# A decode step of attention and a gated feed-forward: which engine issues the loads

## The chip, the cores and the metric

The kernel runs on one core of a Trainium2 chip. The core has TensorE (PE, matrix products), VectorE (DVE), ScalarE (ACT), GpSimd (POOL) and SyncE (SP), which run side by side and wait for each other through semaphores, and 16 DMA engines, which move data between main memory (HBM) and the on-chip memory. Any of SP, ACT and POOL can issue a transfer. The metric is the device time of one execution in microseconds (us).

## The reference

One token (batch 1, width 512) goes through two branches that are mixed by a gate: attention with 32 query heads over a cache of 8 key and value heads, 32768 positions each, and a gated feed-forward of width 1792. All is float32.

```python
B, Sq, D = 1, 1, 512
Hq, Hkv, Sk, Dh = 32, 8, 32768, 128
F = 1792

g = sigmoid((x * gate_w).sum(-1, keepdims=True))
q = (x @ wq).reshape(B, Sq, Hq, Dh).transpose(0, 2, 1, 3)
k, v = repeat(k_cache, 4, axis=1), repeat(v_cache, 4, axis=1)
p = softmax(einsum("bhqd,bhkd->bhqk", q, k) * Dh ** -0.5)
a = einsum("bhqk,bhkd->bhqd", p, v).transpose(0, 2, 1, 3).reshape(B, Sq, Hq * Dh) @ wo
b = (silu(x @ w1) * (x @ w3)) @ w2          # x is A_x
out = g * a + (1 - g) * b
```

## The kernel before, in words

**Units.** The key cache and the value cache are each cut into 16 units. A K unit is a quarter of two heads, a V unit is half of one head; either is 128 partitions by 64 KB, 8.39 MB. I call them K0 to K15 and V0 to V15. The weights wq and wo are of the same size, w1, w3 and w2 have 3.67 MB each; wo is loaded in six parts, of 16, 7, 4, 2, 2 and 1 of its 32 columns of blocks.

**Buffers.** Nearly all of the on-chip memory is in two buffers of one unit each, `big_a` (the buffer number 0 in the code, with halves A0 and A1) and `big_b` (1, with B0 and B1), and in `aside`, three quarters of half a unit. wq goes to `big_a`, K0 and K2 to `big_b`, all other K units to `big_a`. V0 to V11 go to `big_b`, V12 and V14 to `big_a`, V13 and V15 to `big_b`, wo to `big_a`, w2 to the place of `aside`.

**The stages.** First q is computed from wq, spread over TensorE, and turned into `win`. Then a loop over t from 0 to 15 takes in one K unit a turn: ScalarE copies part of the unit to `aside` (`set_aside`, so that `big_a` comes free before the unit is worked up), VectorE transposes it in eight pieces of 128x2048 (L367), TensorE multiplies each piece by q (`scores_part`, L351), ScalarE copies the scores out. After every fourth K unit the scores of two heads are complete: they are transposed on TensorE (`turn`), and `softmax` finds the maximum on VectorE and takes the exponential on ScalarE (`probs`). From t = 4 (`LAG`) on, the same turn also takes V unit v = t - 4: TensorE multiplies it by its probabilities (`values_all`, L452). In the turn t = 3 the products with w1 and w3 are made. After the loop V12 to V15 follow (`load_unit`, `values`, L575), the weights of the heads (`norm`, `place`, `own_head`), then the products with wo (`wide`, L631, and `ff_down`, L662) and with w2 (`down`, on VectorE, L638), and two small stores of the result.

**How the order is made.** The program is written by a small planner of the kernel's own. `pr.add(engine, ...)` appends an operation to the engine's list; it derives from the names that the operation reads and writes which earlier operations it must wait for, and gives it a semaphore to raise. Each engine goes through its own list in the order in which it was written. Every load goes through `load` (L194), except V0 to V11 (`load_values`, L433); both put it on SP's list. A load by `load` raises one of nine semaphores (`lane`), taken in turn.

**TensorE's loop.** The other engines' lists are written out flat, but TensorE runs a real loop over the units. It therefore can't wait for ever higher counts: it waits for a fixed count and takes it off again (`take`). Such a semaphore is a *credit*. The load of V0 to V11 raises the credit "values" by 16 when it has landed, and TensorE does `take("values", 16)` before `values_all`.

**SP's list**, in order: wq, K0, K1, K2, K3, w1, w3, K4, V0, K5, V1, and so on in turn to K15, V11; then V12, V13, V14, V15, w2, the six parts of wo, and one of the two stores. ACT issues the two small rows x and gate_w and the other store. POOL's list: 34 short operations, nearly all of which make masks and constants at the start; the last of these turns the gate into 1 - gate (L302). One more `memset` (L537), in the last turn of the loop, clears `otp`, where the attention's output is laid out for the product with wo.

Of the kernel before, what the change touches and what calls it, by code (L numbers as in the profile page):

```python
# [114 lines left out]
def kernel(  # L115
# [12 lines left out]
    nc = tc.nc  # L128
# [5 lines left out]
    NC = D // P  # L134
# [8 lines left out]
    NP = HKV // 2  # L143
    NH = 4 * NP
# [5 lines left out]
    pr = Program(nc, nc.alloc_semaphore)  # L150
    pr.semaphore("stored")
    pe, dve, act, pool = (
        lambda fn, _e=e, **kw: pr.add(_e, fn, **kw) for e in ("PE", "DVE", "ACT", "POOL")
    )
    V, A, T = nc.vector, nc.scalar, nc.tensor

    def sbuf(name, *shape):
        return nc.alloc_sbuf_tensor(name, [P, *shape], F32)[:]

    fold = sbuf("fold", 32)  # L160
    big = [sbuf("big_a", 2 * R), sbuf("big_b", 2 * R)]
# [19 lines left out]
    otp = kt[1][:, 0:1024].rearrange("p (k c) -> p k c", c=32)  # L181
# [5 lines left out]

    lanes = [0]

    def load(dst, src, writes, over=()):  # L190
        lanes[0] += 1
        lane = f"load{lanes[0] % 9}"
        return pr.add(
            "SP", lambda: nc.sync.dma_start(dst, src), writes=writes, over=[*over, lane], inc=lane, by=16, also=lane,  # L194
        )

    def region(b, z):
# [2 lines left out]

    for i, t in enumerate((x.rearrange("a b n -> (a b) n"), gate_w.rearrange("(o n) -> o n", o=1))):
        pr.add("ACT", lambda i=i, t=t: nc.scalar.dma_start(rows[i][0:1, :], t), writes=[f"row{i}"], inc="row", by=16)
    load(big[0], wq.rearrange("(p c) n -> p (c n)", c=NC), ["A0", "A1"])
    opened = pr.ops["SP"].pop()
    first_load = opened.fn()
    first_load.then_inc(pr.semaphore(opened.inc[0]), opened.inc[1])
# [11 lines left out]
    high, top = sbuf("high", 1), sbuf("top", 32)  # L218
    G = nc.gpsimd
# [45 lines left out]
    def clear(**kw):  # L265
        pe(zeros,
           reads=["acc"], writes=["s"], **kw)
# [15 lines left out]
    for c in range(NC):  # L283
        def part(c=c):
# [18 lines left out]
         reads=["gate0"], writes=["gate1"])  # L303
# [4 lines left out]
    for b in range(2):  # L308
        qt = kt[b][:, 0:512]
        dve(lambda b=b, qt=qt: V.transpose(qt, rows[b]), reads=[f"row{b}"], writes=[f"kt{b}"])  # L310
        for j in range(4):
            w, u = divmod(4 * b + j, 2)
            src = qt[32 * j:32 * j + 32, :].rearrange("p (q c x) -> p x c q", q=4, c=4)[:, 0]
            for e in range(2):
                r, o = 2 * u + e, 16 + 8 * e + 4 * u
                dst = win[32 * r:32 * r + 32, w, :, o:o + 4]
# [5 lines left out]
    kd = k_cache.rearrange("a (w u) s d -> w (a u s d)", u=2).rearrange("w (p m r) -> w m p r", p=P, m=4)  # L322
    vd = v_cache.rearrange("a h (e p n) d -> (a h) e p (n d)", e=2, p=P)

    def where(t):
        return 1 if t in (0, 2) else 0

    def load_keys(t):
        b = where(t)
        load(big[b], kd[t // 4, t % 4], ["AB"[b] + str(z) for z in range(2)])  # L330

# [1 line left out]
    extra = big[1][:, 2 * NC * F:2 * R].rearrange("p (n r) -> p n r", n=NB)  # L335

    def set_aside(t):
        src, key = region(where(t), 1).rearrange("p (n r) -> p n r", n=NB), "AB"[where(t)] + "1"
        act(lambda: A.copy(spare, src[:, :, 32:128]), reads=[key], writes=["wo"])  # L339
        if t == LAG - 1:  # L340
            act(lambda: A.copy(extra, src[:, :, 0:32]), reads=[key], writes=["extra"], over=["B1"])

    def window(t, z):
        return act(
            lambda: A.copy(winc, win[:, t // 4, :, 16 - 16 * z:48 - 16 * z]),  # L345
            reads=[("win", t // 4, r) for r in range(4)], writes=["winc"], credit="windows",
        )
# [30 lines left out]
    def scores_out(t):  # L378
        o = act(
            lambda: A.copy(sb[:, :, :, t % 4], ps_s.rearrange("p (n i) -> p n i", i=32)),  # L380
            reads=["s"], writes=[("sb", t % 4)], credit="scores",
        )
        return o
# [14 lines left out]
    def softmax(w):  # L398
        banks = [f"f{f}" for f in range(4)]

        dve(lambda: V.tensor_reduce(mt[:, 0:8], turned.rearrange("p (n q) -> p q n", q=8), axis=AX.X, op=ALU.max),  # L401
            reads=banks, writes=["mt"])
        for k in range(4):
            dve(lambda k=k: V.transpose(mtt[0:32, 32 * k:32 * k + 32], mt[32 * k:32 * k + 32, :]),  # L404
                reads=["mt"], writes=[("mtt", k)])
        dve(lambda: V.tensor_reduce(high[0:32, :], mtt[0:32, :], axis=AX.X, op=ALU.max),
            reads=[("mtt", k) for k in range(4)], writes=["high"])
        for k in range(4):
            dve(lambda k=k: V.transpose(top[32 * k:32 * k + 32, :], high[0:32, :].to_broadcast([32, 32])),  # L409
                reads=["high"] + ["otp"] * (w == NP - 1 and k == 3), writes=[("top", k)])  # L410
        dve(lambda: V.tensor_tensor(  # L411
            turned.rearrange("p (n q) -> p n q", q=8), turned.rearrange("p (n q) -> p n q", q=8),
            top[:, 0:8].unsqueeze(1).to_broadcast([P, 256, 8]), op=ALU.subtract,
        ), reads=[("top", k) for k in range(4)], writes=banks)

        act(lambda: A.copy(mark, ones[:, 0:1]), reads=["ones"], writes=["mark"])
        for u in range(2):
            act(lambda u=u: A.activation(  # L418
                prob[u][:, 0:1024].rearrange("p (y n q) -> p n y q", y=16, q=4),
                turned.rearrange("p (n y u q) -> p n y u q", n=16, y=16, u=2)[:, :, :, u],  # L420
                AF.Exp, scale=SCALE,
            ), reads=[*banks, "mark"], writes=[("prob", u)], over=["row0", "row1"])
# [6 lines left out]


    def load_values(s):
        return pr.add(
            "SP", lambda: nc.sync.dma_start(big[1], vd[s // 2, s % 2]), writes=["B0", "B1"], over=["extra"],  # L433
            credit="values", by=16,
        )

    def weights(s):
        u, e = s // 2 % 2, s % 2
        return act(
            lambda: A.copy(  # L440
                pv[:, 0:512].rearrange("p (y r) -> p y r", r=64),
                prob[u][:, 0:1024].rearrange("p (y e r) -> p y e r", e=2, r=64)[:, :, e],
            ), reads=["pvpad", ("prob", u)], writes=["pv"], over=["o"], credit="weights",
        )
# [13 lines left out]
    def values_loop(vt, wt, credits):  # L458
        pe(values_all, reads=["B0", "B1", "pv", "pvpad"], writes=["o"], credits=(*credits, (vt, 16), (wt, 1)), loop=True)
# [12 lines left out]
    def load_hidden():  # L472
        for z, t in enumerate((w1, w3)):
            load(big[1][:, z * NC * F:(z + 1) * NC * F], t.rearrange("(p c) f -> p (c f)", c=NC), [f"B{z}"])
# [28 lines left out]
    def store(e, src, key, inc):  # L503
        i, q = (0, nc.scalar) if e == "ACT" else (1, nc.sync)
        pr.add(e, lambda: q.dma_start(outs[2 * i:2 * i + 2, :], src[31 + 64 * i:33 + 64 * i, :]),
               reads=[key], writes=[("out", i)], inc=inc, by=16)

    load_keys(0)
    vals = {}
    first = window(0, 0)  # L510
    for t in range(NH):
        v = t - LAG
        set_aside(t)
        scores(t, 0, first)
        scores(t, 1, window(t, 1))
        out_op = ((scores_out(t), 1),)
        if v < 0:
            clear(loop=True, credits=out_op)
        if t == LAG - 1:
            load_hidden()  # L520
        if t + 1 < NH:
            load_keys(t + 1)
            first = window(t + 1, 0)
        if v >= 1:
            own(v - 1)
        if t % 4 == 3:
            turn(v >= 0, out_op if v >= 0 else ())
        if v >= 0:
            values_loop(vals.pop(v), weights(v), () if t % 4 == 3 else out_op)
            clear(loop=True)  # L530
        if t == LAG - 1:
            hidden_products()
        if v + 1 >= 0 and t + 1 < NH:
            vals[v + 1] = load_values(v + 1)

        if t == NH - 1:
            pool(lambda: G.memset(otp, 0.0), writes=["otp"], over=["kt1"])  # L537
        if t % 4 == 3:
            softmax(t // 4)
        if t % 4 == 0 and t > 0:  # L540
            total(t // 4 - 1)
        if t == LAG:
            hidden()
# [3 lines left out]
    def norm():  # L547
        pe(lambda: T.matmul(pm[0][:, 0:32], ones, sums, start=True, stop=True),  # L548
           reads=["ones"] + [("sums", w) for w in range(NP)], writes=["m0"])
        dve(lambda: V.reciprocal(recip, pm[0][:, 0:32]), reads=["m0"], writes=["recip"])  # L550
        dve(lambda: V.tensor_mul(mine, recip, mask), reads=["recip", "mask"], writes=["mine"])
        dve(lambda: V.tensor_reduce(weight[:, 0:1], mine, axis=AX.X, op=ALU.add), reads=["mine"], writes=["weight"])
        dve(lambda: V.tensor_scalar(
            share, here, weight[:, 0:1], gate[:, 0:1], op0=ALU.mult, op1=ALU.mult,
        ), reads=["here", "weight", "gate0"], writes=["share"])
# [34 lines left out]
    def load_unit(b, s):  # L590
        load(big[b], vd[s // 2, s % 2], ["AB"[b] + str(z) for z in range(2)])

    load_unit(0, 12)
    load_unit(1, 13)
    norm()
    own(11)
    place(0)
# [38 lines left out]
    def down(ks):  # L636
# [9 lines left out]
        reads=[("each", 0), ("each", 1), "otp"], writes=["lay"])  # L646
# [36 lines left out]
    a, b, c, d = flips  # L683
# [68 lines left out]
```

## Time and profile before

| | |
|---|---|
| median of the runs | 691.72 us (691.6 to 691.84, 2 runs) |
| the profiled execution | 691.36 us |
| its span, first to last instruction | 689.6 us |
| read from HBM | 296.23 MB, 430 GB/s over the span |
| TensorE's mean granted clock | 0.80 |

The profile is of one execution. Its page gives the busy time of each engine, the span in 40 equal slices (each digit is the busy share of a slice in tenths), the DMA queues, and the chain of work that ended last. In a table by stretches stand the busy time of each engine, the granted TensorE clock, the share of time in which the 16 DMA engines were busy, and the GB/s they moved. In a timeline a row begins with its start and its length in us; `SPq` is the queue of SyncE, and `DMA_DIRECT2D` there is the issuing of a load, not the transfer; in brackets stands how long the engine had been idle and what ended that. In a row of a group, the numbers behind `|` are the busy time and the mean in ns of one instruction. A DMA list has how many loads of a kind there were and, last in the row, the median time from issue to landing, all 16 engines done.

### The profile page before, as it was taken

The numbers are of one execution on the slowest core, as the hardware profiler recorded it, in microseconds if no ns is written. First come the engines' busy times: TensorE is split into PE (matmuls) and PEld (weight loads), VectorE is DVE, ScalarE is ACT, GpSimd is POOL, SyncE is SP. The second block draws the span as 40 slices with busy tenths as digits, with TensorE's granted clock in tenths as the row PEclk, the third lists the DMA queues.
The fourth block names the chain that finished last, engine by engine and source line by source line (L and its number), as shares of the span: only waits on it lengthen the run. The fifth ranks groups of instructions, "written<-read, shape, count | busy, mean of one in ns | idle before, by whom it ended". The sixth has DMA issues, their size and how long they took to land. (4 is left out here: it accounts for less than half of the span.)

```text
span 689.6 us, 5698 instructions
## 1 busy us (share of the span) xinstructions
PE 397.5 (58%) x2430; PEld 95.0 (14%) x2430; DVE 368.5 (53%) x229; ACT 134.6 (20%) x113; POOL 8.1 (1%) x34
## 2 busy tenths in 40 slices
PE   1537777556473556666374646556484645754577
PEld 0101111201010110201010100201010101311112
DVE  0049998394635627494735637493725537620017
ACT  0143223232303121220303131220303131100000
POOL 4000000000000000000000000000000000000000
PEclk9969999968787777758777876977786777777779
DMA  9999999999999999999999999999999999999997
GB/s 396 450 430 426 426 413 443 431 445 452 426 430 430 430 426 441 456 430 430 430 430 426 437 460 430 430 430 430 426 433 456 437 426 426 433 431 430 442 421 321
DMA packets 6068, 296.34 MB, mean 430 GB/s; under 512 B 678, under 2 KB 682, under 8 KB 1068
## 3 DMA queue, kind: packets, MB, share of 16 engines
q1 hardware_dynamic: 6052, 296.23, 99.3%
q8 instruction: 5, 0.08, 0.0%
q14 instruction: 3, 0.02, 0.0%
q10 hardware_dynamic: 8, 0.01, 0.0%
HBM read 296.23 MB, written 0.00 MB: 430 GB/s over the span
## 5 line engine op out<-in xcount | busy, mean ns | idle before, releaser
L367 DVE STREAM_TRANSPOSE aside<-big_a 128x2048 f32<-128x2048 f32 x41 | 94.3, 2299 | 168.8 <-DMA big_a<-in_A_k_cache_dram 168.8
L351 PE MATMUL ps<-aside,winc 128*32 128x512 f32 x512 | 94.4, 817 | 147.6 <-PEq L689 146.8
L351 PE MATMUL ps<-kt,winc 128*32 128x512 f32 x512 | 92.9, 805 | 62.1 <-PEq L689 62.1
L452 PE MATMUL ps<-big_b,pv 128*32 128x512 f32 x768 | 94.5, 648 | 17.5 <-PEq L689 17.5
L339 ACT COPY aside<-big_a 128x6144 f32<-128x6144 f32 x14 | 74.4, 5313 | 153.5 <-DMA big_a<-in_A_k_cache_dram 153.5
L367 DVE STREAM_TRANSPOSE kt<-aside 128x2048 f32<-128x2048 f32 x32 | 73.3, 2292 | 15.8 <-PE ps L351 15.8
L367 DVE STREAM_TRANSPOSE kt<-big_a 128x2048 f32<-128x2048 f32 x28 | 63.6, 2270 | 0.0
L380 ACT COPY sb<-ps 128x512 f32<-128x512 f32 x16 | 17.1, 1069 | 157.2 <-PE ps L351 157.2
L351 PEld LDWEIGHTS ps<-aside,winc 128*32 128x32 f32 x512 | 13.3, 124 | 217.9 <-issue 217.9
L452 PEld LDWEIGHTS ps<-big_b,pv 128*32 128x32 f32 x768 | 27.5, 119 | 86.7 <-issue 86.7
L367 DVE STREAM_TRANSPOSE aside<-aside 128x2048 f32<-128x2048 f32 x16 | 36.3, 2270 | 0.0
L584 DVE TENSOR_TENSOR sb<-ps,own_b 128x512 f32<-128x512 f32 x2 | 1.4, 692 | 60.4 <-PE ps L575 60.4
L351 PEld LDWEIGHTS ps<-kt,winc 128*32 128x32 f32 x512 | 13.2, 122 | 143.2 <-issue 143.2
L575 PE MATMUL ps<-big_b,probs 128*32 128x512 f32 x128 | 18.1, 727 | 18.2 <-DMA big_b<-in_A_v_cache_dram 18.2
L345 ACT COPY winc<-win 128x128 f32<-128x128 f32 x32 | 9.8, 307 | 76.6 <-PE ps L351 76.6
L575 PE MATMUL ps<-big_a,probs 128*32 128x512 f32 x128 | 16.8, 683 | 11.0 <-DMA big_a<-in_A_v_cache_dram 11.0
L615 PE MATMUL ps<-win,ones 128*128 128x512 f32 x42 | 22.9, 639 | 0.0
L263 PE MATMUL ps<-acc 128*128 128x512 f32 x34 | 20.0, 670 | 3.5 <-POOL acc L220 2.6
L367 DVE STREAM_TRANSPOSE aside<-big_b 128x2048 f32<-128x2048 f32 x7 | 16.1, 2297 | 11.0 <-DMA big_b<-in_A_k_cache_dram 11.0
L401 DVE TENSOR_REDUCE mt<-turned 128x8 f32<-128x2048 f32 x4 | 9.2, 2292 | 22.7 <-PE turned L390 22.7
L425 DVE TENSOR_REDUCE sums<-probs 128x8 f32<-128x2048 f32 x4 | 15.3, 3823 | 2.1 <-ACT probs L418 2.1
L390 PE MATMUL turned<-ident,sb 128*128 128x128 f32 x64 | 11.2, 348 | 4.6 <-PEq L689 4.6
(93 smaller groups left out, 186.5 us busy)
## 6 DMA issues: line engine op xcount, KB each, us to landing
big_b<-in_B_w_dram SPq DMA_DIRECT2D x2, 3584.0 KB, 20.7
big_a<-in_A_wo_dram SPq DMA_DIRECT2D x1, 4096.0 KB, 28.4
aside<-in_B_w_dram SPq DMA_DIRECT2D x1, 3584.0 KB, 38.2
big_a<-in_A_wo_dram SPq DMA_DIRECT2D x1, 1792.0 KB, 32.3
big_a<-in_A_wo_dram SPq DMA_DIRECT2D x1, 1024.0 KB, 34.3
big_a<-in_A_wo_dram SPq DMA_DIRECT2D x2, 512.0 KB, 35.4
big_a<-in_A_wo_dram SPq DMA_DIRECT2D x1, 256.0 KB, 35.9
big_a<-in_A_k_cache_dram SPq DMA_DIRECT2D x14, 26.2
```

The lines of the kernel that those rows point to most:

```text
L263: return T.matmul(ps_s, acc[:, 0:P], acc, start=True, stop=False, skip_group_check=True)
L339: act(lambda: A.copy(spare, src[:, :, 32:128]), reads=[key], writes=["wo"])
L345: lambda: A.copy(winc, win[:, t // 4, :, 16 - 16 * z:48 - 16 * z]),
L351: ins = T.matmul(ps_s[32 * g:32 * g + 32, :], winc[:, c, :], kt[c % 2][:, 512 * g:512 * g + 512], start=False, stop=False, skip_group_chec ...
L367: k = dve(lambda d=dst, s=src: V.transpose(d, s), reads=[key], writes=[f"kt{c % 2}"], over=["kt0"] * (t >= LAG and (z, c) == (1, 1)), cred ...
L380: lambda: A.copy(sb[:, :, :, t % 4], ps_s.rearrange("p (n i) -> p n i", i=32)),
L390: ins = T.transpose(pf[f][:, P * a:P * a + P], sb[:, 4 * f + a].rearrange("p i m -> p (i m)"), ident)
L401: dve(lambda: V.tensor_reduce(mt[:, 0:8], turned.rearrange("p (n q) -> p q n", q=8), axis=AX.X, op=ALU.max), reads=banks, writes=["mt"])
L425: dve(lambda: V.tensor_reduce(sums[:, 8 * w:8 * w + 8].rearrange("p (u q) -> p u q", u=2), probs[:, :, 0:1024].rearrange("p u (n q) -> p u ...
L452: ins = T.matmul(ps_o[32 * t:32 * t + 32, :], pv[:, o:o + 32], big[1][:, n * P:(n + 4) * P], start=((z, g) == (0, 0)), stop=((z, g) == (1, ...
L575: ins = T.matmul(ps_o[32 * t:32 * t + 32, :], prob[u][:, o:o + 32], vt[:, n * P:(n + 4) * P], start=((e, z, g) == (0, 0, 0)), stop=((e, z, ...
L615: return T.matmul(bank[:, 0:n], ones, win.rearrange("p w c n -> p (w c n)")[:, 0:n], start=True, stop=True)
```

## The change

`load` gets a parameter that says which engine issues, POOL unless SP is asked for. wq and K0 stay with SP; the other 40 loads go to POOL's list, in the same order as they had on SP's. The semaphores are named by engine and still taken in turn out of nine.

V0 to V11 no longer raise the credit "values" themselves. Each raises a semaphore of its own, `vload`, by 16. A new operation on POOL's list, `hand_over(s)`, waits until `vload` has reached 16 * s + 16 and then raises "values" by 16. It stands in the turn where the products of V unit s are written: behind the load of K(t + 1), where there is one, and ahead of the load of V(s + 1), where there is one.

The `memset` of `otp` moves from the last turn of the loop to behind the loads of V12 and V13 on POOL's list, and the last `softmax` no longer waits for it.

```diff
-    def load(dst, src, writes, over=()):
+    def load(dst, src, writes, over=(), e="POOL"):
         lanes[0] += 1
-        lane = f"load{lanes[0] % 9}"
+        lane = f"{e}{lanes[0] % 9}"
+        q = {"POOL": nc.gpsimd, "SP": nc.sync}[e]
         return pr.add(
-            "SP", lambda: nc.sync.dma_start(dst, src), writes=writes, over=[*over, lane], inc=lane, by=16, also=lane,
+            e, lambda: q.dma_start(dst, src), writes=writes, over=[*over, lane], inc=lane, by=16, also=lane,
         )
...
-    load(big[0], wq.rearrange("(p c) n -> p (c n)", c=NC), ["A0", "A1"])
+    load(big[0], wq.rearrange("(p c) n -> p (c n)", c=NC), ["A0", "A1"], e="SP")
...
-        load(big[b], kd[t // 4, t % 4], ["AB"[b] + str(z) for z in range(2)])
+        load(big[b], kd[t // 4, t % 4], ["AB"[b] + str(z) for z in range(2)], e="SP" if t == 0 else "POOL")
...
-                reads=["high"] + ["otp"] * (w == NP - 1 and k == 3), writes=[("top", k)])
+                reads=["high"], writes=[("top", k)])
...
     def load_values(s):
-        return pr.add(
-            "SP", lambda: nc.sync.dma_start(big[1], vd[s // 2, s % 2]), writes=["B0", "B1"], over=["extra"],
-            credit="values", by=16,
-        )
+        pr.add("POOL", lambda: nc.gpsimd.dma_start(big[1], vd[s // 2, s % 2]), writes=["B0", "B1"], over=["extra"],
+               inc="vload", by=16)
+
+    def hand_over(s):
+        return pool(lambda: G.wait_ge(pr.semaphore("vload"), 16 * s + 16), reads=["B0", "B1"], credit="values", by=16)
...
-            values_loop(vals.pop(v), weights(v), () if t % 4 == 3 else out_op)
+            values_loop(hand_over(v), weights(v), () if t % 4 == 3 else out_op)
             clear(loop=True)
         if t == LAG - 1:
             hidden_products()
         if v + 1 >= 0 and t + 1 < NH:
-            vals[v + 1] = load_values(v + 1)
-
-        if t == NH - 1:
-            pool(lambda: G.memset(otp, 0.0), writes=["otp"], over=["kt1"])
+            load_values(v + 1)
+
...
     load_unit(0, 12)
     load_unit(1, 13)
+    pool(lambda: G.memset(otp, 0.0), writes=["otp"], over=["kt1"])
```

More of the change, by code (lines that the diff above doesn't have):

```diff
@@ L508 @@
     load_keys(0)
-    vals = {}
     first = window(0, 0)
```

## The prediction

> **What bounds the kernel now.** I read the page from the top: how busy each engine is, the slices, the DMA queues, then the table by stretches of time.
>
> ```profile
> PE 397.5 (58%) x2430; PEld 95.0 (14%) x2430; DVE 368.5 (53%) x229; ACT 134.6 (20%) x113; POOL 8.1 (1%) x34
> DMA  9999999999999999999999999999999999999997
> q1 hardware_dynamic: 6052, 296.23, 99.3%
> core 0: us, PE busy (x) PEld busy (x) DVE busy (x) ACT busy (x) POOL busy (x), PEclk, DMA share, GB/s
> 20.00:40.00 20.00, 9.05 (x66) 2.72 (x66) 1.31 (x2) 4.86 (x20) 0.19 (x1) 0.91 0.97 417
> 100.00:600.00 500.00, 292.35 (x1774) 67.18 (x1766) 289.98 (x172) 109.49 (x82) 0.95 (x1) 0.77 1.00 435
> 600.00:660.00 60.00, 28.47 (x200) 7.74 (x204) 7.74 (x10) 0.00 (x0) 0.00 (x0) 0.76 0.98 425
> ```
>
> No compute engine passes 58%, while the 16 DMA engines are at 99.3% of the span on the one queue that SP fills, and from 100 to 600 us they move 435 GB/s at a share of 1.00. The kernel is its transfers: 296.23 MB at 435 GB/s are 681.0 us of the span of 689.6. The other 8.6 us are all that any better issuing could win (1.2%), and some of them, the first issue and the last result, stay whatever is done. A big load (K, V, wq, wo) is 8.39 MB (128 rows of 64 KB), 8.39 / 0.435 = 19.3 us.
>
> A queue that never empties hides when its loads are issued. So the question is how early each load is issued; the DMA list gives the median from issue to landing.
>
> ```profile
> big_a<-in_A_wq_dram SPq DMA_DIRECT2D x1, 21.9
> big_a<-in_A_k_cache_dram SPq DMA_DIRECT2D x14, 26.2
> big_b<-in_A_v_cache_dram SPq DMA_DIRECT2D x14, 26.8
> ```
>
> wq found an idle queue: 21.9 - 19.3 = 2.6 us is what a load from SP takes beyond its bytes. K and V need 26.2 and 26.8 us because they wait behind the load before them, 6.9 and 7.5 us. That wait is the **cover**: a load may be issued so much later before an engine stands still. One of the 16 DMA engines may be a row ahead of another (64 KB at an eighth of 19.3 us, 2.4 us), so I count on 4.5 us.
>
> **The change, part by part.** Nothing is computed differently. POOL issues 40 of the 42 loads (15 K, 16 V, w1, w3, w2, six parts of wo), all but wq and K0: 279.5 MB of the 296.2.
>
> *Who issues.* SP loses some 0.33 us for each issue (row below), on an engine that does nothing else: worth nothing. POOL has 8.1 us of work in the span, so it is free to take them.
>
> *K1, the first load on POOL.* It now stands behind POOL's set-up, whose last piece waits for the gate.
>
> ```profile
> 31.63 0.33 SPq L194 DMA_DIRECT2D big_a<-in_A_k_cache_dram  x1
> 32.18 0.19 POOL L302 TENSOR_SCALAR gate<-gate 128x1 f32<-128x1 f32 x1 [15.41 <-ACT gate L301]
> 43.25 2.31 DVE L367 STREAM_TRANSPOSE aside<-big_b 128x2048 f32<-128x2048 f32 x1 [9.34 <-DMA big_b<-in_A_k_cache_dram]
> ```
>
> POOL comes to K1 at 32.4 instead of 31.6, and K0 lands at 43.25: 11 us of cover, cost 0.
>
> *POOL's price for a load.* No load here is issued from POOL, so it is bounded. Beyond SP's price: not below -0.3 (SP's own 0.33 us saved), at most another 2.6, all that SP's load needs beyond its bytes. The nearest row is SP's issue; I take twice it, 0.66 us. Even 2.6 is under the 4.5 of cover, so for a load in the queue it costs 0.
>
> *The order on POOL.* An engine goes through its instructions in order, so each new wait on POOL holds the loads behind it. In the loop POOL now has: K(t+1), hand-over(v), V(v+1), K(t+2)... Hand-over(v) waits until V(v) has landed. Behind it stands V(v+1), which writes the same buffer and must wait for TensorE's use of V(v) anyhow. K(t+1) stands ahead of it, and is issued 6.9 us before V(v) lands. So in the loop the new wait holds nothing. TensorE gets the value semaphore one hop later; the first value product shows what hides that.
>
> ```profile
> 130.42 0.33 SPq L433 DMA_DIRECT2D big_b<-in_A_v_cache_dram  x1
> 150.16 0.33 SPq L194 DMA_DIRECT2D big_a<-in_A_k_cache_dram  x1
> L452 PE MATMUL ps<-big_b,pv x768: 589/592/1063, 160.1 to 595.8; 128*32 128x512 f32 x192
> ```
>
> V0, issued at 130.42, lands at about 157.2 (26.8 later); the products begin at 160.1, since scores stand ahead of them. A hop below 0.7 us is hidden there, and would else only eat V's cover.
>
> *The end of the loop.* Here the order does bite. The last turn (t = 15) has no K(16) and no V(12) to load; it adds hand-over(11) alone. Only after the loop come the loads by `load_unit`, V12 first. So V12 stands **behind hand-over(11)**, hence behind the landing of V11. On SP nothing stood between.
>
> ```profile
> 554.55 0.33 SPq L433 DMA_DIRECT2D big_b<-in_A_v_cache_dram  x1
> 562.83 2.31 DVE L367 STREAM_TRANSPOSE aside<-big_a 128x2048 f32<-128x2048 f32 x1 [16.62 <-DMA big_a<-in_A_k_cache_dram]
> 575.24 0.33 SPq L194 DMA_DIRECT2D big_a<-in_A_v_cache_dram  x1
> 596.42 0.33 SPq L194 DMA_DIRECT2D big_b<-in_A_v_cache_dram  x1
> 605.01 7.79 PE L575 MATMUL ps<-big_a,probs 128*32 128x512 f32 x64
> 612.88 0.33 SPq L194 DMA_DIRECT2D big_a<-in_A_v_cache_dram  x1
> 620.75 1.94 PE L575 MATMUL ps<-big_b,probs 128*32 128x512 f32 x8 [7.94 <-DMA big_b<-in_A_v_cache_dram]
> ```
>
> The rows are the issue of V11, the landing of K15 (its first transpose), the issues of V12 and V13, V12's products, the issue of V14, the landing of V13. K15 lands at 562.8, V11 behind it at 562.8 + 19.3 = 582.1. V12 was issued at 575.24, 6.9 us before; now not before 582.1, when no load is queued at all: V13 needs big_b, which TensorE still reads. **The DMA engines run dry once.** V12 then pays what wq paid. Before, it landed at 620.75 - 19.3 = 601.4. Now: 582.1, 0.14 to wake (chain of work, below), 0.66 for POOL, 21.9 as for wq: 604.8. That is +3.4 us; with POOL's bounds and a wake of 0 to 0.95 (POOL's longest instruction in the loop, the memset below) +2.2 to +6.2.
>
> The Trainium skill ("DMA: Bandwidth & Descriptors", Latency and other measured facts) puts the first byte of a GpSimd-issued load at about 1 us and of an SP-issued one at about 0.6. No run here shows it yet; by it POOL's extra would be 0.4, an estimate from that page, and the sum +3.1.
>
> *Is it given back later?* V12's products began at 605.01, after other work of VectorE, so a landing at 604.8 delays no issue behind it; but every later load follows the one before it without a gap:
>
> ```profile
> 640.02 0.14 issue
> 649.20 28.43 DMA big_a<-in_A_wo_dram
> 685.73 0.70 DVE acc L653
> 649.20 2.70 SPq L194 DMA_DIRECT2D big_a<-in_A_wo_dram  x6
> 584.11 0.95 POOL L537 MEMSET kt<- 128x1024 f32 x1 [551.74 <-PE ps L351]
> 673.69 1.89 DVE L645 TENSOR_REDUCE kt<-sb 128x32 f32<-128x1024 f32 x1
> ```
>
> V13 lands at 620.75, V14 at 640.02 (19.3 later), and wo's first part, issued at 649.20, at 677.63, though its 4.19 MB take 9.6 us: it queued for 18.8. So a shift at V12 goes through to the end undiminished, and the six issues of wo may take POOL 18 us before they cost anything. The `memset` of otp moves from 584 to behind V13's issue, some 597, and is wanted at 673.69: 0. The wait for it that leaves the last softmax had long ended: 0.
>
> Sum against the profiled execution: 691.36 (span 689.6 and 1.8 around it) + 3.4 = 694.8. The median, 691.72, is 0.36 above that execution, so I forecast 695.0.
>
> **The rivals.**
>
> *No dry stretch: 691.7.* Everything above without V12's wait. It would need POOL to issue V12 past a wait that stands ahead of it, or the change not to do what it says (loads still issued early). The order in the code speaks against it. Here too belongs a small win from the 8.6 us: at most 1.2%, and nothing shows what POOL would mend of them.
>
> *The engines move POOL's loads a little slower: slower than before.* SP's loads run at 435 GB/s in the body, but the same engines showed 425 from 600 to 660 and 417 from 20 to 40, so the rate isn't fixed. If POOL's 279.5 MB ran at 425: 657.6 instead of 642.5 us, +15.1, and with the dry stretch 710.2. At 417 it would be 723. Since every microsecond of transfer is on the path, 428 GB/s (a loss of 1.6%) is enough for 2%. Against it: the loads keep their 64 KB rows and the engines. The Trainium skill (the same page and section) speaks for it: it says that DMA engines 7 and 15 are usually slower, and guesses at the place in SBUF of the descriptors that GpSimd writes; before has no such load to show it.
>
> *POOL is held while VectorE works: far slower.* K loads are issued into a run of transposes.
>
> ```profile
> L367 DVE STREAM_TRANSPOSE kt<-aside 128x2048 f32<-128x2048 f32 x32 | 73.3, 2292 | 15.8 <-PE ps L351 15.8
> ```
>
> A hold over one transpose, 2.3 us, with POOL's 0.66 stays under the 4.5 of cover. Over three it is 6.9 + 0.66 - 4.5 = 3.1 us late, 15 times (K1 to K15), +46, so about 741; it decides from two transposes on. Against it: POOL's work and VectorE's don't use the same data, and nothing on POOL reads a tensor. The Trainium skill ("SBUF — State Buffer", SBUF: two separate sides) says that VectorE locks GpSimd out of writing descriptors only in its two-port modes; 2048 columns in 2292 ns, above 1 ns each, don't look like such a mode, so by that rule the hold would not come.
>
> **How the numbers follow.** Forecast (dry once, same rate) 0.65, its own range 693.5 to 698. No dry stretch 0.11, 690 to 693. Slower transfers 0.17, from 699 to 723, over half of it past 2%. Held POOL 0.07. A change within 2% (13.8 us, to 705.6) is about what a measurement of this kernel can't tell from none. Within it: 0.65 + 0.10 + 0.07 of the slower transfers = 0.82; slower 0.10 + 0.07 = 0.17; faster by 2% would need more than the 8.6 us there are, 0.01. The range goes from 690 to 708, taking in a rate down to 426; the upper rivals leave 0.15 outside.
>
> **What the profile of the changed kernel would show.** V12's issue, now a POOL row, at 582 to 583 instead of 575.24, its landing about 22 to 23 us later instead of 26.2, and one dip of the DMA share near 583, none elsewhere. From 100 to 560 us 435 GB/s at 1.00 as before; anything lower there is the second rival. Every other K load still issued some 12 us after its predecessor landed, with 25 us or more to landing; if the K loads land more than 19.3 us after the load ahead, the third. K1's issue at about 32.4. V13 landing near 624 and wo's first part near 681. The forecast is wrong if V12 is issued at 575, if POOL needs much more than 0.66 us beyond SP, or if the rate in the body moves by over half a per cent.

## The result, and the profile after

The changed kernel takes 701.9 us (median of 2 runs; 691.7 before), a ratio of 1.0147 with a 95% interval from 1.0104 to 1.0191. Four more runs in a later comparison gave 700.7 us, 1.0128 (1.0110 to 1.0145). So it is slower by 9 to 10 us; the forecast was 695.0, 3.4 us slower, with a range from 690 to 708.

On the page of the changed kernel, the first lines and the queues:

```profile
span 700.7 us, 5711 instructions
DMA  9997999999999999999999999999999998999997
q0 software_dynamic: 5696, 279.45, 92.3%
q1 hardware_dynamic: 292, 16.78, 5.7%
L195 POOL DMA_DIRECT2D big_a<-in_A_k_cache_dram x14 | 7.6, 542 | 242.2 <-PE ps L352 227.4
```

POOL's loads have a queue of their own, q0; wq and K0 stay in SP's, q1. In the DMA row all slices are at 9 but the last and two more, the 4th (53 to 70 us) and the 34th (578 to 596). The table by stretches shows them, with before's rows for two of the stretches first:

```profile
60.00:80.00 20.00, 13.87 (x77) 2.98 (x74) 18.46 (x9) 6.71 (x4) 0.00 (x0) 1.00 1.00 433
580.00:590.00 10.00, 8.20 (x40) 3.93 (x43) 3.31 (x3) 1.58 (x3) 0.95 (x1) 0.53 1.07 465
```

and the changed kernel's:

```profile
60.00:80.00 20.00, 15.20 (x87) 3.45 (x84) 19.37 (x9) 7.01 (x5) 0.54 (x1) 1.00 0.75 318
100.00:560.00 460.00, 276.35 (x1645) 61.09 (x1646) 268.47 (x154) 100.35 (x75) 12.66 (x24) 0.76 1.00 434
580.00:590.00 10.00, 5.69 (x32) 0.65 (x24) 7.34 (x4) 0.35 (x1) 0.53 (x1) 0.73 0.78 308
```

The last two columns count: DMA share and GB/s. From 100 to 560 us hardly anything has changed (434 GB/s at 1.00; before, 435 from 100 to 600). The DMA engines stand still for a quarter of the 20 us from 60 on (5 us), and for a fifth of the 10 us from 580 (2.2 us). The second is the dry stretch that was forecast; the first was not. The timeline of the changed kernel at both places:

```profile
1.99 0.33 SPq L195 DMA_DIRECT2D big_b<-in_A_k_cache_dram  x1
33.34 0.73 POOL L195 DMA_DIRECT2D big_a<-in_A_k_cache_dram  x1
50.84 2.31 DVE L368 STREAM_TRANSPOSE aside<-big_b 128x2048 f32<-128x2048 f32 x1 [15.90 <-DMA big_b<-in_A_k_cache_dram]
64.19 0.54 POOL L195 DMA_DIRECT2D big_b<-in_A_k_cache_dram  x1 [30.13 <-PE ps L352]
...
588.27 0.53 POOL L195 DMA_DIRECT2D big_a<-in_A_v_cache_dram  x1 [27.47 <-DMA big_b<-in_A_v_cache_dram]
602.20 0.53 POOL L195 DMA_DIRECT2D big_b<-in_A_v_cache_dram  x1 [13.40 <-PE ps L455]
630.95 1.93 PE L575 MATMUL ps<-big_b,probs 128*32 128x512 f32 x8 [12.62 <-DMA big_b<-in_A_v_cache_dram]
```

*At the end of the loop.* V12 is issued at 588.27, and its row says that POOL waited for a V load into big_b: V11, which landed at 587.67 by the completion records (they tell when the last of the 16 engines reports the end of a load). V12 lands at 610.35, 22.7 us after V11 where it had been 19.3.

*At the start.* K0 lands at 50.8 instead of 43.2, although SP issued it at the same time (1.99 us). K2 needs K0's buffer and goes out at 64.19 instead of 55.69. K1 had landed at 62.87 (before: 62.53), so the queue was empty. The same two issues in the kernel before:

```profile
1.98 0.33 SPq L194 DMA_DIRECT2D big_b<-in_A_k_cache_dram  x1
55.69 0.33 SPq L194 DMA_DIRECT2D big_b<-in_A_k_cache_dram  x1
```

The DMA list of the changed kernel says the same in three rows:

```profile
big_a<-in_A_wq_dram SPq DMA_DIRECT2D x1, 21.9
big_b<-in_A_k_cache_dram SPq DMA_DIRECT2D x1, 48.8
big_b<-in_A_k_cache_dram POOLq DMA_DIRECT2D x1, 22.4
```

wq as before; K0 48.8 us from issue to landing (before 41.2); K2 22.4 us, what a load takes that finds an idle queue.

The delay of each landing against before, from the completion records, makes the sum:

```
        before    after    later by
K0       43.2      50.8      7.6
K1       62.5      62.9      0.3
K2       81.8      86.6      4.8
K3      101.1     106.2      5.1
V11     582.1     587.7      5.6
V12     601.4     610.4      8.9
V13     620.7     630.9     10.2
wo end  687.4     697.5     10.2
span    689.6     700.7     11.1
```

5.1 us come in at the start, 3.4 at V12, 1.3 at V13, 0.5 on the long way between, and 0.9 behind the last landing (each is rounded). The last of these belongs to that one execution: in the second profile of the changed kernel the span ends 2.2 us after the last landing, as before.

### The profile page after: what moved, and what is told of

The parts are those of the page before. It is cut to its first block, busy times and chain, and to the rows that moved or that the text cites. A ratio compares the mean times of both kernels' runs of the same rounds, so it can differ in the third digit from the quotient of the medians.

```text
span 700.7 us, 5711 instructions
## 1 busy us (share of the span) xinstructions
PE 405.6 (58%) x2430; PEld 96.1 (14%) x2430; DVE 368.7 (53%) x229; ACT 134.7 (19%) x113; POOL 29.3 (4%) x74
## 5 line engine op out<-in xcount | busy, mean ns | idle before, releaser
L352 PE MATMUL ps<-kt,winc 128*32 128x512 f32 x512 | 95.1, 823 | 58.2 <-PEq L690 58.2
L455 PE MATMUL ps<-big_b,pv 128*32 128x512 f32 x768 | 96.0, 657 | 17.4 <-PEq L690 17.4
L575 PE MATMUL ps<-big_b,probs 128*32 128x512 f32 x128 | 18.4, 738 | 21.9 <-DMA big_b<-in_A_v_cache_dram 21.9
L402 DVE TENSOR_REDUCE mt<-turned 128x8 f32<-128x2048 f32 x4 | 9.2, 2292 | 22.7 <-PE turned L391 22.7
L195 POOL DMA_DIRECT2D big_a<-in_A_k_cache_dram x14 | 7.6, 542 | 242.2 <-PE ps L352 227.4
```

Of the source, the lines that this page charges most:

```text
L195: e, lambda: q.dma_start(dst, src), writes=writes, over=[*over, lane], inc=lane, by=16, also=lane,
L352: ins = T.matmul(ps_s[32 * g:32 * g + 32, :], winc[:, c, :], kt[c % 2][:, 512 * g:512 * g + 512], start=False, stop=False, skip_group_chec ...
L455: ins = T.matmul(ps_o[32 * t:32 * t + 32, :], pv[:, o:o + 32], big[1][:, n * P:(n + 4) * P], start=((z, g) == (0, 0)), stop=((z, g) == (1, ...
L575: ins = T.matmul(ps_o[32 * t:32 * t + 32, :], prob[u][:, o:o + 32], vt[:, n * P:(n + 4) * P], start=((e, z, g) == (0, 0, 0)), stop=((e, z, ...
```

## The experiments

**The order at V12.** My theory: V12 stands behind hand-over(11). The rivals: POOL itself is late, or the later step at V13 has another cause. First, the changed kernel with V12's load written ahead of the hand-over:

```diff
+    def load_unit(b, s):
+        load(big[b], ...)
...
             first = window(t + 1, 0)
+        else:
+            load_unit(0, 12)
...
-    def load_unit(b, s):
-        load(big[b], ...)
-
-    load_unit(0, 12)
     load_unit(1, 13)
```

> Edit: the changed kernel with the load of V12 written into the last turn of the loop, ahead of hand-over(11) on POOL's list; wq and K0 stay on SP. Theory (order): V12 is issued some 6.9 us before V11 lands, lands 19.3 us after it, V13 19.3 us later again, and 4.6 us go (3.4 at V12, 1.2 at V13, which landed 20.5 us after V12): before + 5 to 6. Rival: only the 3.4 at V12 goes, and the 1.2 at V13 have another cause and stay: before + 6.5 to 7.5. Rival: a load from POOL into the buffer that K units used is late whatever the order: no change against the changed kernel, before + 10.

Measured: 695.6 us, 1.0052 (1.0036 to 1.0069). Its timeline:

```profile
567.85 5.31 ACT L340 COPY aside<-big_a 128x6144 f32<-128x6144 f32 x1 [15.92 <-DMA big_a<-in_A_k_cache_dram]
581.34 0.53 POOL L195 DMA_DIRECT2D big_a<-in_A_v_cache_dram  x1 [21.29 <-PE ps L352]
601.49 0.53 POOL L195 DMA_DIRECT2D big_b<-in_A_v_cache_dram  x1 [19.62 <-PE ps L455]
625.78 6.52 PE L580 MATMUL ps<-big_b,probs 128*32 128x512 f32 x32 [8.19 <-DMA big_b<-in_A_v_cache_dram]
```

K15 lands at 567.85, V13 at 625.78: three loads (V11, V12, V13) in 57.9 us, 19.3 each. V12 goes out at 581.34, and POOL's wait for it is now for TensorE (the buffer), not for V11. Both steps are gone, the 3.4 and the 1.3. The time came out under what I expected: 3.9 above before in place of 5 to 6, which is 5.0 us less than the changed kernel's 700.7 and 6.3 less than its first two runs. The profiled execution was the longest of the four (696.8; the others 694.5 to 696.3), so the loss at the start may be smaller in some executions; that isn't shown.

Second, the same wait on the other engine: the kernel before, with all its loads on SP, and SP handing the value credit on.

```diff
     def load_values(s):
-        return pr.add("SP", lambda: nc.sync.dma_start(...), ..., credit="values", by=16)
+        pr.add("SP", lambda: nc.sync.dma_start(...), ..., inc="vload", by=16)
+
+    def hand_over(s):
+        return pr.add("SP", lambda: nc.sync.wait_ge(pr.semaphore("vload"), 16 * s + 16),
+                      reads=["B0", "B1"], credit="values", by=16)
...
-            values_loop(vals.pop(v), ...)
+            values_loop(hand_over(v), ...)
```

> Edit: the kernel before, all loads on SP, with the hand-over alone: V0 to V11 raise a semaphore of their own, and SP waits for it and raises the credit, in the same place of its list (V12 behind hand-over(11)). Theory (order, not engine): SP issues V12 only when V11 has landed, the engines run dry, V12 lands 22 us and V13 20.5 us after the load ahead: before + 3 to 5. Rival (the dry stretch is POOL's slow start of a load): before, within 1 us.

Measured: 695.3 us, 1.0053 (1.0036 to 1.0069), 3.6 above before. Rows of its timeline:

```profile
582.43 0.33 SPq L194 DMA_DIRECT2D big_a<-in_A_v_cache_dram  x1
624.76 7.54 PE L576 MATMUL ps<-big_b,probs 128*32 128x512 f32 x56 [11.56 <-DMA big_b<-in_A_v_cache_dram]
```

a row of its stretches:

```profile
580.00:590.00 10.00, 8.01 (x36) 3.94 (x40) 3.25 (x3) 1.58 (x3) 0.95 (x1) 0.50 0.79 315
```

and one of SP's waits (total, times, longest):

```profile
SPq L436 <- DMA big_b<-in_A_v_cache_dram: 95.9, 12, 25.3
```

SP issues V12 at 582.43, when V11 has landed (582.34); V13 lands at 624.76, 42.4 us after V11 for two loads of 19.3. The DMA share dips to 0.79 as on POOL. SP waits 95.9 us in its 12 hand-overs, and only the last costs anything: V11 still lands 0.2 us after its time in the kernel before. So the dry stretch is the order, not the engine. POOL adds little: after V11's landing it needs 0.60 us to issue, SP 0.09, and V12 then lands 22.1 us after its issue, on SP 21.8.

**The start.** Theory A: K0 in SP's queue and K1 in POOL's share the DMA engines, so K0 lands late. Theory B: a first load from POOL costs something of its own. I tried to remove the second queue by putting wq and K0 on POOL too:

```diff
-    load(big[0], wq..., ["A0", "A1"], e="SP")
-    opened = pr.ops["SP"].pop()
+    load(big[0], wq..., ["A0", "A1"], e="POOL")
+    opened = pr.ops["POOL"].pop()
     first_load = opened.fn()
...
     tc.compile()
+    load(big[1], kd[0, 0], ["B0", "B1"])
...
-    load_keys(0)
```

> Edit: the changed kernel, but wq and K0 are issued by POOL as well, so that every load is in one queue; V12 still stands behind hand-over(11). Theory A (two queues): in the changed kernel K0 on SP's queue and K1 on POOL's share the 16 DMA engines row by row, so K0 lands at 50.8 us instead of 43.2, and K2, which needs K0's buffer, comes 1.3 us after K1 has landed: the engines run dry. In one queue K0 lands at 43 to 44, K2 at 82 to 83, the two stretches before V12 cost nothing, and the time is 5 us below the changed kernel: before + 4.5 to 6. Theory B (POOL's loads have a price of their own at first, whatever the queue): wq or K1 is late by as much, and the time stays within 1.5 us of the changed kernel.

Measured: 701.0 us, 1.0136 (1.0119 to 1.0153), the time that theory B had named. But the timeline shows that something else happened:

```profile
1.32 0.67 POOL L195 DMA_DIRECT2D big_a<-in_A_wq_dram  x1 [0.80 <-PEq L210]
24.35 0.52 ACTq L203 DMA_DIRECT2D probs<-in_A_x_dram  x1
24.78 0.53 POOL L195 DMA_DIRECT2D big_b<-in_A_k_cache_dram  x1 [22.80 <-POOLq L210]
```

Behind the program's opening the engines begin only at 24 us; before, ACT's first issue was at 1.99. wq is issued ahead of the program's opening, and with wq on POOL the opening waits until it has landed, at 23.7. K0 is issued into an empty queue and lands at 48.3, 5.1 us later than before: 1.0 because wq landed later, 4.1 for a new dry stretch. From K0 on, the loads do land 19.3 us apart (K1 67.6, K2 87.0, K3 106.3). So the run took one loss away and put another in its place, and its time says nothing on A and B. The same with V12 first:

> Both edits together: all loads in POOL's queue, V12 ahead of hand-over(11). If the two dry stretches are all of the loss: before, within 1 us (690.9 to 692.9), the loads landing 19.3 us apart from K0 to V15. If a load from POOL costs something of its own that the queue doesn't hide: 2 us or more above before even so.

Measured: 696.5 us, 1.0069 (1.0052 to 1.0086). The expectation failed for the same reason; it is 4.5 below the run without V12 first, the price of the order once more.

To set A against B without POOL, I took the kernel before and moved K1 alone to ACT, which has a queue of its own as well:

```diff
-    def load(dst, src, writes, over=()):
+    def load(dst, src, writes, over=(), e="SP"):
...
+    load(big[0], kd[0, 1], ["A0", "A1"], e="ACT")
     for b in range(2):
         act(lambda b=b: A.copy(rows[b], pf[b]), ...)
...
-            load_keys(t + 1)
+            if t:
+                load_keys(t + 1)
```

> Edit: the kernel before, all loads on SP, but K1 alone is issued by ACT, at the place in its list behind the gate's sigmoid (about 32 us). No load is on POOL. Theory A (two queues share the engines row by row): from 32 us K0 gets half the engines, lands at 50 to 51 us instead of 43.2, K1 still at 62.5; K2 is issued at 63 to 64, after K1 has landed, and lands 22.5 to 24 us after K1: before + 3.5 to 5.5. Theory B (what cost time at the start was POOL's late or slow first load): K0 lands at 43 to 44 and the time is before, within 1 us.

Measured: 696.4 us, 1.0082 (1.0056 to 1.0108). Its timeline:

```profile
31.66 0.36 ACTq L195 DMA_DIRECT2D big_a<-in_A_k_cache_dram  x1
50.39 5.31 ACT L341 COPY aside<-big_b 128x6144 f32<-128x6144 f32 x1 [12.86 <-DMA big_b<-in_A_k_cache_dram]
62.80 0.33 SPq L195 DMA_DIRECT2D big_b<-in_A_k_cache_dram  x1
```

and of its stretches:

```profile
60.00:80.00 20.00, 15.68 (x88) 3.44 (x84) 19.71 (x10) 7.01 (x5) 0.00 (x0) 1.00 0.88 367
```

K1 goes out as early as in the kernel before (31.66), no load is on POOL, and K0 lands at 50.4 all the same; K2 is issued at 62.80, after K1 has landed (62.42), and the DMA share falls to 0.88. Theory B is out: two queues are enough. The packet records of the changed kernel show how (start times in us; a row is one packet of 64 KB, and behind its last row of a load each engine sends a packet of 4 bytes, its completion mark):

```
36.40 to 37.15   15 rows of K0 (SP's queue)
38.31 to 39.56   16 rows of K1 (POOL's queue)
40.73 to 41.98   16 rows of K0
43.14 to 44.39   16 rows of K1
45.55            the last row of K0, on one engine that lags
46.05 to 46.81   15 completion marks of K0
47.97            a row of K1 on that engine
50.38            its completion mark, the last of K0
```

By the times each engine takes a row (2.42 us) of the one queue and then one of the other. Hardly any rate is lost (419 GB/s from 40 to 60 us, before 423), and K1 lands 0.3 us later than before. But on the last engine K0's rows, and the mark behind them, wait for three rows of K1 (38.31, 43.14 and 47.97): 3 x 2.42 = 7.3 us of the 7.6. With ACT's queue the records show the same alternation, three rows of K1 ahead of each engine's mark.

Then the switch of queues at another place, with V12 first. With K1 on SP too, POOL begins with K2, which is issued much later in its forerunner's transfer:

```diff
-        load(big[b], ..., e="SP" if t == 0 else "POOL")
+        load(big[b], ..., e="SP" if t < 2 else "POOL")
```

> Edit: the changed kernel with V12 ahead of hand-over(11), and K1 issued by SP like K0, so that POOL begins with K2. The two queues then meet at K1 and K2, where K2 is issued only 6.9 us before K1 has landed (K1 was issued 11 us before K0 landed). Theory A: K1 lands about 6 us late, at 68 to 69, K2 on time at 82; K3, which needs K1's buffer, is issued at 81 to 82.5, just as K2 lands: a dry stretch of 0 to 2.5 us, before + 0 to 3, so 1 to 4 us less than with the switch one load earlier (695.6). Theory B (POOL's first loads cost something wherever they stand): before + 4, as with K1 on POOL.

Measured: 692.6 us, 1.0014 (1.0005 to 1.0024). Its timeline:

```profile
56.16 0.73 POOL L195 DMA_DIRECT2D big_b<-in_A_k_cache_dram  x1 [23.91 <-PE ps L352]
65.18 5.31 ACT L340 COPY aside<-big_a 128x6144 f32<-128x6144 f32 x1 [1.54 <-DMA big_a<-in_A_k_cache_dram]
78.70 0.53 POOL L195 DMA_DIRECT2D big_a<-in_A_k_cache_dram  x1 [21.82 <-PE ps L352]
```

K1 lands at 65.2, 2.6 us late, about one row of K2 and not the 6 that I expected. By the packet records K2's first rows start at 60.5, 4.4 us after its issue, when every engine has begun its last row of K1; only K1's marks still wait, each for one row of K2. K3 goes out at 78.70, with K2 in the queue until 82.1. Nothing runs dry, and 3 us are gone against the switch one load earlier (695.6). Theory B had said no difference.

All 42 loads on POOL, this time with wq inside the program (the lines with `opened` and `first_load` removed), and V12 first:

> Edit: all 42 loads on POOL, V12 ahead of hand-over(11), and wq issued inside the program instead of ahead of its opening: with wq from POOL ahead of it, the opening waited for wq to land (K0 was issued at 24.8 us). Theory A: wq is issued at 2 to 3 us, K0 right behind it in the same queue, no load waits for an empty queue, all land 19.3 us apart to the end: before + 1 to 2.5, all of it the later first issue. Theory B (a load from POOL has a price that the queue doesn't hide): before + 4 or more.

Measured: 693.2 us, 1.0023 (1.0014 to 1.0033). Its timeline:

```profile
1.97 0.67 POOL L195 DMA_DIRECT2D big_a<-in_A_wq_dram  x1 [1.46 <-POOLq L206]
2.64 0.53 POOL L195 DMA_DIRECT2D big_b<-in_A_k_cache_dram  x1
```

and a row of its DMA list:

```profile
big_a<-in_A_wq_dram POOLq DMA_DIRECT2D x1, 22.1
```

wq goes out 1.2 us later than from SP ahead of the opening (0.81) and lands 22.1 us after, where SP's took 21.9: 1.4 us later in all. The time is 1.6 above before. So POOL as the issuer of everything costs its later first issue and hardly anything else.

Last, the other way to keep the two queues apart: K1 on POOL as in the change, V12 first, and K1 made to wait for `win`, so that it is issued **later**.

```diff
-        load(big[b], ..., e="SP" if t == 0 else "POOL")
+        load(big[b], ..., over=[("win", 3, r) for r in range(4)] if t == 1 else (), e="SP" if t == 0 else "POOL")
```

> Edit: the changed kernel with V12 ahead of hand-over(11), and K1 on POOL held back until ScalarE has filled win, so that it is issued at about 37 us instead of 33: a later issue of a load is the only difference to the run with V12 first (695.6). Theory A (two queues share the engines): K0 has less left to move when K1 joins, lands at 46 to 49 instead of 50.7; K2 is issued at 58.5 to 61.5, ahead of K1's landing at 62.5 to 63; the dry stretch before K2 goes wholly or nearly: 2 to 4 us less than with V12 first alone, before + 0.5 to 2. Theory B (K1 on POOL comes late): K1 is later still, so the time is the same or higher.

Measured: 693.6 us, 1.0029 (1.0016 to 1.0041), about 2 us less than with V12 first alone, and 2.2 above before, a little over the 0.5 to 2 that I expected. Its timeline:

```profile
38.21 0.73 POOL L195 DMA_DIRECT2D big_a<-in_A_k_cache_dram  x1 [5.08 <-ACT win L318]
45.72 5.31 ACT L340 COPY aside<-big_b 128x6144 f32<-128x6144 f32 x1 [7.49 <-DMA big_b<-in_A_k_cache_dram]
58.41 0.53 POOL L195 DMA_DIRECT2D big_b<-in_A_k_cache_dram  x1 [19.47 <-PE ps L352]
81.91 2.31 DVE L368 STREAM_TRANSPOSE aside<-big_b 128x2048 f32<-128x2048 f32 x1 [0.52 <-DMA big_b<-in_A_k_cache_dram]
```

K1 is issued 5 us later than in the changed kernel, and K0 lands 5 us earlier (45.7, still 2.5 later than before: on the last engine one row of K1 goes ahead of K0's mark). K2 goes out 6 us earlier (58.41) and lands at 81.9, as in the kernel before. In this execution the loss at the start is gone. Its runs lie between 691.8 and 696.1, wider than those of the others, so the dry stretch may come back in some of them; that I didn't trace.

In that comparison the changed kernel itself ran again:

> The changed kernel as it is, for an interval of its own beside the others: before + 9.5 to 10.5.

Measured: 700.7 us, 1.0128 (1.0110 to 1.0145), a little under what I expected; in its profile K2 lands 22.9 us after K1, V12 22.8 after V11 and V13 20.5 after V12.

No version beats the kernel before. The nearest is the one with K1 on SP and V12 first, 1.1 us above it.

## Why the prediction was right or wrong

*The number.* The measured 701.9 us lies in the range of 690 to 708, but not for the reason that I gave. My forecast, one dry stretch at an unchanged rate, had its own range of 693.5 to 698, and the time lies above it. The range went up to 708 for slower transfers, which didn't come; that it holds the result is luck. (The sum also gives 695.1 where I wrote 695.0.)

*What bounds the kernel.* Right. The body runs at 434 GB/s with POOL's loads as with SP's, and the stretches in which no load is queued show in the time.

*The order at the end of the loop.* Right in kind and size: V12 issued behind V11's landing, forecast +3.4 (0.14 to wake, 0.66 for POOL, 2.6 for an idle queue), measured 3.4 at V12. The parts came out a little otherwise: the wake on POOL was 0.60 in place of 0.14, the rest of POOL's price about 0.2 in place of 0.66. One was too low and the other too high by as much, so that the sum fits this well is luck as well. The 0.4 us between the two ways of issuing, my estimate by the first-byte figures of the Trainium skill ("DMA: Bandwidth & Descriptors", Latency and other measured facts), stands beside a measured 0.2 (22.1 against 21.9 for wq).

*What follows V12.* Missed: a further 1.3 us at V13. I had carried a shift at V12 to the end "undiminished", and not asked whether it grows. The four profiles with a dry V12 have the step (1.0 to 1.3); in those without, V13 comes 0 to 0.5 us late. The packet records point to a cause that I haven't tested. The 16 engines don't finish a load together; in the kernel before the last was 0.5 us behind the first at wq and 1.6 at K0, after a 16 KB instruction fetch at 34.1 us. K0 landed 20.5 us after wq, 1.2 more than 19.3, and the loads behind it again 19.3 apart. In the changed kernel the last mark comes 1.8 us behind the first at V11, 0.7 at V12, behind the dry stretch, and 1.7 at V13; between these a 16 KB instruction fetch at 614.5 is followed by one row of V13 that takes 2.97 us instead of 2.42. So a dry stretch may level the engines, and the fetch open the lag anew; a run without the fetch would be needed to show it.

*K1, "cost 0".* **This is the step that failed.** I asked whether K1 would be issued early enough for itself, found 11 us of cover, and stopped. The harm was to the load ahead of it: the earlier K1 is issued, from another queue, the more of its rows go ahead of the last rows of K0. I had read from the DMA list that a load waits behind the load before it, which is so in the one queue that SP fills, but I hadn't asked what becomes of that order when there are two queues. It is 5.1 of the 10.2 us (4.2 of 9.2 in the second profile). The long cover, which I counted as safety, let in the rows: with 6.8 us of it (K2 from POOL) the load ahead came 2.6 us late in place of 7.6, and the time was 1.1 us above before in all. One of the signs that I had named, no dip of the DMA share but the one near 583, did fail; none of those by which I would have called the forecast wrong looked at the start.

*The rivals.* Slower transfers: not so, 434 GB/s. So no rate was lost to the slower DMA engines of which the Trainium skill ("DMA: Bandwidth & Descriptors", Latency and other measured facts) speaks. The 425 and 417 GB/s that I took for a rate that isn't fixed stood beside DMA shares of 0.98 and 0.97: for the most part those engines stood still, they weren't slower. A POOL held by VectorE: not so, from K5 on K loads are issued 6.2 us or more ahead of the landing before them, and land 19.2 to 19.3 us behind it while VectorE is busy for 268 of the 460 us from 100 on, most of it with transposes. That agrees with the rule of the Trainium skill ("SBUF — State Buffer", SBUF: two separate sides) on the two-port modes. No dry stretch: excluded by the row of V12.

*Costs put at nothing.* The hop of the value credit, the six issues of wo from POOL (0.53 us each in place of 0.33 to 0.43), the moved `memset` (602.72 to 603.69, ahead of nothing): small, by the two versions at 692.6 and 693.2 us. Both hold all of these costs, and the first is only 1.1 us above before.

## What to carry to other kernels

Where the transfers bound a kernel, take the list of loads in their new order and ask of each two things: which wait now stands ahead of it on its engine, above all at a loop's end, where the load that usually goes ahead is missing; and which load of another queue is in flight beside it. A load that is issued early in a second queue didn't wait its turn here; it made the load ahead late, and the cost appeared at the load that needed that buffer. Moving the loads to another engine gained nothing here, since SP, which issued them, never was what they waited for.

## What the runs showed of the hardware that I had not expected

- Two queues share the DMA engines row by row (2.42 us for 64 KB), whether the second is POOL's or ACT's: K0 landed 7.1 to 7.6 us late, and K1, from the second queue, within 0.4 us of its time before.
- The completion mark of a load waits too: with K2 from POOL all rows of K1 had begun ahead of K2's, and K1 still landed 2.6 us late, behind one row of K2.
- A load issued from POOL ahead of the program's opening held the opening until it had landed (23.7): the first issue behind it came at 24.35 us instead of 1.99. The same load from SP doesn't (issued at 0.81, landed at 22.7).
- A load from POOL into an idle queue takes 22.1 us against 21.9 from SP; its issue keeps POOL 0.53 us (0.6 to 0.73 the first times), SP 0.33.
